# Loading the decay rates as one packet and spreading their logarithm by a matmul with ones, with k first on SyncE's queue

## The chip, the cores and the metric

The kernel runs on one core of a Trainium2 chip. The core has five engines that run side by side, each with its own instruction stream: TensorE (PE, matmul), VectorE (DVE), ScalarE (ACT), GpSimd (POOL) and SyncE (SP, which here only issues DMAs). They wait for each other through semaphores. The metric is the device time of one execution in microseconds (us), as the median of several runs. A profile is one further execution, recorded instruction by instruction.

## The reference

The program is a block-wise linear attention with a decay rate per head (`lam`, 8 numbers between 0.97 and 0.99), and behind it a two-layer network with the "snake" activation. Shapes: q, k and v are 4 x 8 x 768 x 64 (batch, head, position, dimension) in float32; the network takes 3072 tokens of 512 to 2048 and back to 512.

```python
Dmask = np.where(rel >= 0, lam[:, None, None] ** rel[None, :, :], 0.0)
for b in range(nb):                      # blocks of 64 positions
    intra = einsum('bhic,bhjc->bhij', qb, kb) * Dmask
    intra = einsum('bhij,bhjd->bhid', intra, vb)
    inter = einsum('bhid,bhde->bhie', qb * lam_pow, kv_state)
    out[:, :, sl] = intra + inter
    kv_state = lam_block * kv_state + einsum('bhsd,bhse->bhde', kb * rev_pow, vb)
h = x @ w_in                             # x: attention output, tokens x 512
s = np.sin(alpha * h)
g = h + s * s / (alpha + 1e-09)
return g @ w_out
```

## The kernel before

The kernel works on blocks of 128 positions (24 of them, six per batch) and on chunks of 512 tokens (six). Powers of lam are not put into a mask. They are multiplied into q and k: q of position p by lam^p, k by lam^-p, so that the mask that remains is 0 or 1. The factors are made once at the start. GpSimd writes the exponents (`E_i`, cast to `E_f`, lines 412 to 418), ScalarE takes `Ln` of lam (`lnlam`, line 438), VectorE multiplies the two (`lnL`, line 441), and ScalarE takes `Exp` into the tables `Lp`, `Lk` and `Lq` (lines 443 to 449). lam is loaded with a step of zero over 128 partitions (line 404), so every partition holds all 8 values. Three small activations load function tables: line 438 that of `Ln`, line 440 (`warm`) that of `Exp`, line 450 that of `Sin`, which the network needs.

The start, for the first four blocks, goes like this. SyncE's queue loads k and q (line 324, a helper that all loads share), then v, then the first quarter of `w_in` (`ws`). VectorE, and GpSimd for one of eight pieces, scale k (line 485) and q (line 468) into bf16. TensorE transposes them (lines 539 for q and 566 for k), ScalarE and VectorE copy the transposes out of PSUM (lines 544 and 577), TensorE makes the scores (line 618), VectorE masks them (`Sm`, line 629), and TensorE multiplies them with v (line 765) and adds the running state (`Zd`, lines 654, 672 and 785). The first matmuls of the network (line 862, then 828) come at about 19 us, and from there on attention blocks and network units are interleaved.

The order of the instructions on each engine is a fixed table of numbers (`_Plan.ORDER`): each number is an operation in the order in which the code makes them, and each engine works its row off from left to right, waiting on semaphores where an operation depends on another engine. In TensorE's row a pair such as `(64, 128)` is no operation of the kernel: it stands for 64 matmuls of 128 columns on a constant tile (`spin`, line 1140, whose operand is memset by VectorE on line 419 into a part of `Xs`). Their result is not used.

The lines on lam:

```python
load(lam_bc[:, :], bass.AP(lam.tensor, 0, [[0, 128], [1, H]]), "lam", 0.1, "lam", "SP", ...)
op("ACT", lambda e: e.activation(lnlam[:, :], lam_bc[:, :], ACTF.Ln), 0.25, ["lam"], ["lnlam"])
op("ACT", lambda e: e.activation(warm[:, :], lnlam[:, 0:1], ACTF.Exp, scale=0.0), 1.5, ["lnlam"], ["warm"])
op("DVE", lambda e: e.tensor_tensor(lnL[:, :, :], E_f[:, :, :], lnlam_b, ALU.mult), 0.46, ["E_f", "lnlam"], ["lnL"])
```

## Time and profile before

| what | value |
|---|---|
| time, median of 3 runs (lowest, highest) | 210.52 us (209.93, 210.64) |
| profiled execution: its time / its span from first to last instruction | 209.95 us / 208.2 us |
| busy share of TensorE, VectorE, ScalarE, GpSimd | 96%, 81%, 71%, 64% |
| granted TensorE clock, mean | 1.0 |
| moved by DMA | 34.40 MB in 83222 packets |

Times in the rows below are in us from the first instruction of the span, durations of one instruction in ns where a row says so. `PEld` is TensorE's loading of weights, `SPq` and `ACTq` are the issuing of DMAs by SyncE and ScalarE. In a row of the timeline the first number is the start and the second how long the group took from its first start to its last end; `x64` merges 64 instructions alike, and the bracket says how long the engine sat idle before it and what ended that.

### The profile page before, as it was taken

What the parts mean: (1) busy time and instruction counts of PE and PEld (TensorE: products, weight loads), DVE (VectorE), ACT (ScalarE), POOL (GpSimd) and SP (SyncE); (2) the same over time, 40 slices, a digit from 0 to 9 for tenths busy, and PEclk for the clock granted to TensorE, in tenths of its full rate; (3) what the DMA queues carried; (4) which work ended last, traced back from release to release, by engine and by line L of the source; (5) the groups of instructions that cost most, each with busy time, mean ns of one, the idle gap of its engine ahead of it and who ended that gap; (6) DMA issues with size and microseconds to landing.
All of it is one profiled execution on the core that took longest, in us unless ns stands there. A gap on an engine that the chain in (4) does not pass through costs nothing.

```text
span 208.2 us, 4897 instructions
## 1 busy us (share of the span) xinstructions
PE 200.0 (96%) x1972; PEld 136.8 (66%) x1972; DVE 168.5 (81%) x296; ACT 147.7 (71%) x270; POOL 132.4 (64%) x140
## 2 busy tenths in 40 slices
PE   6988999999997999998999999999999999999995
PEld 6756444557765877665657576665667666667994
DVE  2898567886989999987988979899798866767854
ACT  5658999448998999976979776898765579734300
POOL 6065689834968987954796850958851695585400
DMA  4999999999899999799997999380300004000324
GB/s 133 323 315 216 202 255 214 213 238 245 197 179 230 232 250 248 154 215 206 208 245 156 242 271 185 67 194 26 136 0 3 0 32 169 3 0 20 128 94 165
DMA packets 83222, 34.40 MB, mean 165 GB/s; under 512 B 59632, under 2 KB 80384, under 8 KB 83200
## 3 DMA queue, kind: packets, MB, share of 16 engines
q1 hardware_dynamic: 78544, 29.24, 62.5%
q0 software_dynamic: 3696, 3.67, 10.9%
q10 hardware_dynamic: 960, 1.19, 1.9%
q8 instruction: 15, 0.25, 0.5%
q14 instruction: 7, 0.06, 0.1%
HBM read 27.28 MB, written 6.29 MB: 161 GB/s over the span
## 4 chain that ended last, share of the span: by engine, by line
PE 79%; DVE 9%; ACT 4%; DMA 3%; SPq 2%; issue 1%; ACTq 1%; POOL 0%
PE bank L828 28%; PE bank L981 26%; PE bank L862 7%; PE bank L893 6%; PE bank L722 3%; PE bank L618 3%; DMA v<-in_v_dram 3%; SPq L324 2%; DVE gT L880 2%; DVE Sm L629 2%; DVE gT L845 2%; PE bank L700 1%; DVE w L936 1%; PE bank L654 1%; ACT Zd L672 1%; PE bank L662 1%
## 5 line engine op out<-in xcount | busy, mean ns | idle before, releaser
L828 PE MATMUL bank<-xT,w 128*128 128x512 bf16 x296 | 70.9, 380 | 1.0 <-ACT kept L1018 0.7
L845 DVE SCALAR_TENSOR_TENSOR gT<-u,rinv,bank 128x512 bf16<-128x512 bf16 x74 | 53.6, 744 | 18.2 <-ACT u L842 14.1
L838 ACT ACTIVATE t<-bank,alpha 128x512 bf16<-128x512 f32 x74 | 49.9, 683 | 19.9 <-PE bank L828 19.0
L828 PEld LDWEIGHTS bank<-xT,w 128*128 128x128 bf16 x296 | 27.8, 98 | 28.8 <-DVE gT L845 1.4
L959 POOL TENSOR_TENSOR gT<-gT 128x512 bf16<-128x512 bf16 x28 | 32.1, 1158 | 14.1 <-DVE Xs L959 8.9
L842 ACT ACTIVATE u<-t 128x512 bf16<-128x512 bf16 x57 | 35.2, 628 | 1.5
L843 POOL TENSOR_TENSOR u<-t 128x512 bf16<-128x512 bf16 x17 | 17.6, 1040 | 25.7 <-ACT t L838 25.7
L629 DVE TENSOR_TENSOR Sm<-bank,mask 128x1024 bf16<-128x1024 f32 x24 | 28.9, 1216 | 3.0 <-PE bank L618 1.1
L862 PE MATMUL bank<-xT,w 128*128 128x256 bf16 x176 | 21.6, 273 | 1.0 <-DVE gT L880 1.0
L880 DVE SCALAR_TENSOR_TENSOR gT<-u,rinv,bank 128x256 bf16<-128x256 bf16 x44 | 18.9, 474 | 4.2 <-ACT u L876 3.5
L959 POOL TENSOR_TENSOR Xs<-gT 128x512 bf16<-128x512 bf16 x19 | 21.8, 1162 | 0.3 <-DVE gT L845 0.3
L981 PE MATMUL bank<-w,gT 128*128 128x256 bf16 (+1 forms) x168 | 20.1, 268 | 0.0
L872 ACT ACTIVATE t<-bank,alpha 128x256 bf16<-128x256 f32 x44 | 18.5, 471 | 2.0 <-PE bank L862 1.7
L981 PE MATMUL bank<-ws,gT 128*128 128x256 bf16 x160 | 19.6, 273 | 0.0
L981 PE MATMUL bank<-w,Xs 128*128 128x256 bf16 (+1 forms) x168 | 19.5, 268 | 0.0
L478 POOL TENSOR_TENSOR qk<-q,Lq 128x512 bf16<-128x512 f32 x17 | 18.2, 1077 | 2.0 <-DMA q<-in_q_dram 2.0
L497 POOL TENSOR_TENSOR qk<-k,Lk 128x512 bf16<-128x512 f32 x16 | 17.4, 1090 | 3.3 <-DMA k<-in_k_dram 3.2
L862 PEld LDWEIGHTS bank<-xT,w 128*128 128x128 bf16 x176 | 16.3, 98 | 4.2 <-DVE gT L880 1.8
L981 PEld LDWEIGHTS bank<-w,gT 128*128 128x128 bf16 x168 | 15.9, 98 | 4.1 <-DVE gT L959 0.2
L981 PEld LDWEIGHTS bank<-w,Xs 128*128 128x128 bf16 x168 | 15.6, 98 | 3.3
L981 PEld LDWEIGHTS bank<-ws,gT 128*128 128x128 bf16 x160 | 15.3, 98 | 3.1 <-ACT xT L732 0.4
L893 PE MATMUL bank<-w,gT 128*128 128x512 bf16 x64 | 15.8, 380 | 0.0
(105 smaller groups left out, 266.0 us busy)
## 6 DMA issues: line engine op xcount, KB each, us to landing
k<-in_k_dram SPq DMA_DIRECT2D x24, 256.0 KB, 5.1
q<-in_q_dram SPq DMA_DIRECT2D x12, 512.0 KB, 6.2
v<-in_v_dram SPq DMA_DIRECT2D x24, 256.0 KB, 5.8
out_dram<-osb SPq DMA_DIRECT2D x18, 256.0 KB, 2.6
w<-in_moe_w_out_dram POOLq DMA_DIRECT2D x4, 512.0 KB, 7.8
w<-in_moe_w_in_dram POOLq DMA_DIRECT2D x3, 512.0 KB, 8.1
ws<-in_moe_w_in_dram SPq DMA_DIRECT2D x2, 512.0 KB, 7.5
out_dram<-osb ACTq DMA_DIRECT2D x8, 128.0 KB, 3.7
```

Of the source, the lines that this page charges most:

```text
L478: lambda e, a=a: e.tensor_tensor(qk2[:, j:j + 2, 4 * a:4 * a + 4, :], q32[:, jq, 4 * a:4 * a + 4, :, :].rearrange("p h t d -> p t h d"), b ...
L629: op("DVE", lambda e: e.tensor_tensor(Sm[js][:, :, :], banks[:, 512 * b0:512 * b0 + 1024].rearrange("p (c i) -> p c i", i=128), bass.AP(ma ...
L828: ins = e.matmul(ps[hb][:, c0:c1], w1[:, kc, 128 * m:128 * (m + 1)], xT[x][:, kc, c0:c1], start=(kc == 0 and c0 == lo), stop=(kc == NKC - ...
L838: op("ACT", lambda e: e.activation(t16[ju][:, w], ps[hb][:, w], ACTF.Sin, scale=alpha[:, m:m + 1]), 0.69 if hi - lo == TCH else 0.475, [ba ...
L842: lambda e: (e.activation(u16[ju][:, w], t16[ju][:, w], ACTF.Square) if e is nc.scalar else e.tensor_tensor(u16[ju][:, w], t16[ju][:, w], ...
L845: op("DVE", lambda e: e.scalar_tensor_tensor(out=gT[g][:, m, w], in0=u16[ju][:, w], scalar=rinv[:, m:m + 1], in1=ps[hb][:, w], op0=ALU.mul ...
L862: ins = e.matmul(ps[hb][:, 256 * i:256 * i + 256], w1[:, kc, 128 * (m + i):128 * (m + i + 1)], xT[x][:, kc, lo:lo + 256], start=(kc == 0 a ...
L872: op("ACT", lambda e, i=i: e.activation(t16[ju][:, 256 * i:256 * i + 256], ps[hb][:, 256 * i:256 * i + 256], ACTF.Sin, scale=alpha[:, m + ...
L880: op("DVE", lambda e, i=i: e.scalar_tensor_tensor(out=gT[g][:, m + i, lo:lo + 256], in0=u16[ju][:, 256 * i:256 * i + 256], scalar=rinv[:, ...
L893: ins = e.matmul(ps[ob][:, w], gT[g][:, m, 128 * s4:128 * (s4 + 1)], w2[:, m, w], start=(m == 0), stop=(m == NM - 1),)
L959: e.tensor_tensor(dst, in0, in1, alu), 0, rd, wr))
L981: ins = e.matmul(ps[ob][:, lo + d0:lo + d1], lhs, rhs[:, d0:d1], start=first and p == 0, stop=(p == NM // 2 - 1), skip_group_check=True)
```

## The change

lam is loaded into one partition (`lam_sb`, 1 x 8, one run of 32 bytes), and ScalarE issues that load as its first DMA, ahead of the load of alpha; SyncE's queue then begins with k. `Ln` works on one partition. A matmul of a row of 128 ones (new memset on VectorE) with the 8 logarithms writes them to all 128 partitions of PSUM bank 7, from where VectorE multiplies them with the exponents. Right behind the issue of alpha's load, ScalarE loads one table set that holds both `Ln` and `Exp`, so the `warm` activation for `Exp` goes; the one for `Sin` stays and now reads `lnL`. The fillers at TensorE's start are split into 14, the new matmul and 40. GpSimd casts `E_f` ahead of the mask work instead of behind some of it. A rule on what writes `ws` later in the kernel (line 935) is widened to both halves.

```diff
         "PE": (
-            (64, 128), 58, (5, 512), 60, 54, (11, 128), 38, 56, 52, 61, 66, 64, (1, 128), 68, 69, 74, 77,
+            (14, 128), 32, (40, 128), 59, (5, 512), 61, 55, (11, 128), 39, 57, 53, 62, 67, 65, (1, 128), 69, 70,
...
         "SP": (
-            0, 4, 3, 5, 2, 6, 7, 8, 9, 11, 10, 95, 96, 111, 108, 109, 110, 116, 112, 113, 121, 115, 114, 200,
+            4, 3, 5, 2, 6, 7, 8, 9, 11, 10, 96, 97, 112, 109, 110, 111, 117, 113, 114, 122, 116, 115, 201, 118,
...
-        lam_bc = sb("lam_bc", [128, H], F32)
-        lnlam = sb("lnlam", [128, H], F32)
+        lam_sb = sb("lam_sb", [1, H], F32)
+        lnlam = sb("lnlam", [1, H], F32)
+        ones = sb("ones", [1, 128], F32)
...
-            load(lam_bc[:, :], bass.AP(lam.tensor, 0, [[0, 128], [1, H]]), "lam", 0.1, "lam", "SP", lat=0.8, runs=1)
-            load(alphaT[:, :], bass.AP(moe_alpha.tensor, 0, [[128, NM], [1, 128]]), "alphaT", 0.1, "alphaT", "ACT", lat=2.0, runs=1)
+            load(lam_sb[:, :], bass.AP(lam.tensor, 0, [[H, 1], [1, H]]), "lam", 0.1, "lam", "ACT", lat=0.8, runs=1)
+
+            def load_alpha(e):
+                ins = e.dma_start(alphaT[:, :], bass.AP(moe_alpha.tensor, 0, [[128, NM], [1, 128]]))
+                e.preload_act_table_set("natural_log_exp_and_others")
+                return ins
+
+            op("ACT", load_alpha, 0.1, dma="alphaT", lat=2.0, issue=0.55, runs=1, writes=["alphaT"])
...
-            op("ACT", lambda e: e.activation(lnlam[:, :], lam_bc[:, :], ACTF.Ln), 0.25, ["lam"], ["lnlam"])
-            lnlam_b = bass.AP(lnlam, 0, [[H, 128], [0, 2 * NB + 4], [1, H]])
-            op("ACT", lambda e: e.activation(warm[:, :], lnlam[:, 0:1], ACTF.Exp, scale=0.0), 1.5, ["lnlam"], ["warm"])
+            op("DVE", lambda e: e.memset(ones[:, :], 1.0), 0.1, writes=["ones"])
+            op("ACT", lambda e: e.activation(lnlam[:, :], lam_sb[:, :], ACTF.Ln), 0.25, ["lam"], ["lnlam"])
+            op("PE", lambda e: e.matmul(ps[7][:, 0:H], ones[:, :], lnlam[:, :]), 0.3, ["ones", "lnlam"], [bank(7)])
+            lnlam_b = bass.AP(banks, 512 * 7, [[8 * 512, 128], [0, 2 * NB + 4], [1, H]])
             op("DVE", lambda e: e.tensor_tensor(lnL[:, :, :], E_f[:, :, :], lnlam_b, ALU.mult), 0.46,
-               ["E_f", "lnlam"], ["lnL"])
+               ["E_f", bank(7)], ["lnL"])
...
-            op("ACT", lambda e: e.activation(warm[:, :], lnlam[:, 0:1], ACTF.Sin, scale=0.0), 1.5,
-               ["lnlam", "Lk", "Lq", "Lq4", "Lp"], ["warm"])
+            op("ACT", lambda e: e.activation(warm[:, :], lnL[:, 0, 0:1], ACTF.Sin, scale=0.0), 1.5,
+               ["lnL", "Lk", "Lq", "Lq4", "Lp"], ["warm"])
...
-                        wr = [("T", i, x) for x in m] + ([("ws", 256 * (i // 3))] if i < 4 else [] if i == 4 else keys)
+                        wr = [("T", i, x) for x in m] + ([("ws", 0), ("ws", 256)] if i < 4 else [] if i == 4 else keys)
```

How the change moves instructions is best seen on three engines. On ScalarE, at the very start, before (the two loads of function tables and the `warm` between `Ln` and the first `Exp`):

```order
L324 DMA alphaT<-in_moe_alpha_dram 16x128
L438 ACT_TABLE_LOAD
L438 ACTIVATE lnlam<-lam_bc 128x8
L440 ACT_TABLE_LOAD
L440 ACTIVATE warm<-lnlam 128x1
L445 ACTIVATE Lp<-lnL 128x32
```

and ScalarE at the same place now:

```order
L325 DMA lam_sb<-in_lam_dram 1x8
L408 DMA alphaT<-in_moe_alpha_dram 16x128
L409 ACT_TABLE_LOAD
L446 ACTIVATE lnlam<-lam_sb 1x8 [waits dma_lam]
L453 ACTIVATE Lp<-lnL 128x32 [waits done_DVE]
```

One table load and one activation are gone between `lnlam` and `Lp`, and one DMA issue has come in ahead of the table load that remains. On TensorE, at its start, before (`Xs` is the constant tile of the fillers, `ident,qk` the transposes of q and k):

```order
L1140 MATMUL bank<-Xs 128x128 x64
L539 MATMUL bank<-ident,qk 128x128 x4
L1140 MATMUL bank<-Xs 128x512 x5
L566 MATMUL bank<-ident,qk 128x128 x4
L539 MATMUL bank<-ident,qk 128x128 x4
L1140 MATMUL bank<-Xs 128x128 x11
L453 MATMUL bank<-identf,alphaT 128x16
L539 MATMUL bank<-ident,qk 128x128 x8
```

and TensorE at the same place now, with its waits:

```order
L1148 MATMUL bank<-Xs 128x128 x13
L447 MATMUL bank<-lnlam,ones 128x8 [waits done_ACT]
L1148 MATMUL bank<-Xs 128x128 x40
L547 MATMUL bank<-ident,qk 128x128 [waits done_DVE]
L547 MATMUL bank<-ident,qk 128x128 x3
L1148 MATMUL bank<-Xs 128x512 x5
```

A row with one filler matmul of the same kind stands ahead of the first of these, so it is 14, the matmul that waits for ScalarE, and 40: 54 fillers in place of 64. On SyncE's queue, at its start, before (lam, then the first loads of k and q):

```order
L324 DMA lam_bc<-in_lam_dram 128x8
L324 DMA k<-in_k_dram 128x4x128
L324 DMA q<-in_q_dram 128x4x256
L324 DMA k<-in_k_dram 128x4x128
L324 DMA q<-in_q_dram 128x4x256
```

and SyncE's queue now:

```order
L325 DMA k<-in_k_dram 128x4x128
L325 DMA q<-in_q_dram 128x4x256
L325 DMA k<-in_k_dram 128x4x128
L325 DMA q<-in_q_dram 128x4x256
L325 DMA k<-in_k_dram 128x4x128 x2
```

Every load behind lam's stands one place further ahead; nothing else on this queue has moved.

## The prediction

> **What bounds the kernel now.** I read the page first, for where the time lies at all:

> ```profile
> span 208.2 us, 4897 instructions
> PE 200.0 (96%) x1972; PEld 136.8 (66%) x1972; DVE 168.5 (81%) x296; ACT 147.7 (71%) x270; POOL 132.4 (64%) x140
> PE 79%; DVE 9%; ACT 4%; DMA 3%; SPq 2%; issue 1%; ACTq 1%; POOL 0%
> ```

> TensorE is busy 96% of the span and carries 79% of the chain that ended last. The change touches only the first 8 us, so the question is by how much the first matmul of the network (19 us) moves; behind it TensorE runs nearly without a gap in a fixed order, and a shift there should reach the end.

> Next, the chain of waits within the first 30 us, in order of time (start, length, what):

> ```profile
> 0.81 0.40 SPq L324
> 1.25 0.42 SPq L324
> ...
> 6.35 6.02 DMA v<-in_v_dram
> 12.42 0.62 POOL v L491
> 13.09 0.62 PE bank L654 x8
> ...
> 16.93 1.05 ACT w L393
> 18.81 0.40 PE bank L785 x4
> 19.21 1.75 PE bank L862 x16
> ```

> The head begins with SyncE's issues, one behind the other, the first of them lam's, and then waits for the landing of v's second load. That is a chain of transfers. The second chain that I have to know runs over k, q and the scores; the timeline of the first 16 us shows it:

> ```profile
> 0.80 0.42 ACTq L324 DMA_DIRECT2D alphaT<-in_moe_alpha_dram  x1
> 0.90 0.17 DVE L426 MEMSET mask<- 128x128 bf16 x1 [0.90 <-PEq L1240]
> 1.25 1.28 ACT L438 ACT_TABLE_LOAD   x1 [1.25 <-PEq L1240]
> 1.66 5.60 PE L1140 MATMUL bank<-Xs 128*128 128x128 bf16 x64 [1.66 <-DVE Xs L419]
> 1.72 0.50 SPq L324 DMA_DIRECT2D q<-in_q_dram  x1
> 3.86 0.21 ACT L438 ACTIVATE lnlam<-lam_bc 128x8 f32<-128x8 f32 x1 [1.33 <-DMA lam_bc<-in_lam_dram]
> 4.09 1.28 ACT L440 ACT_TABLE_LOAD   x1
> 4.11 0.29 DVE L441 TENSOR_TENSOR lnL<-E_f,lnlam 128x128 f32<-128x128 f32 x1 [2.36 <-ACT lnlam L438]
> 5.68 0.23 ACT L445 ACTIVATE Lp<-lnL 128x32 f32<-128x32 f32 x1
> 5.95 0.69 DVE L485 TENSOR_TENSOR qk<-k,Lp 128x512 bf16<-128x512 f32 x1 [1.41 <-ACT Lp L445]
> 6.56 0.22 DVE L424 CAST ident<-identf 128x128 bf16<-128x128 f32 x1
> 6.69 1.29 DVE L468 TENSOR_TENSOR qk<-q,Lq 128x512 bf16<-128x512 f32 x2
> 7.43 0.40 PE L539 MATMUL bank<-ident,qk 128*128 128x128 bf16 x4 [0.17 <-DVE qk L468]
> 8.80 1.29 DVE L468 TENSOR_TENSOR qk<-q,Lq 128x512 bf16<-128x512 f32 x2 [0.21 <-DMA q<-in_q_dram]
> 9.90 0.23 PE L453 MATMUL bank<-identf,alphaT 16*128 16x16 f32 x1
> 10.07 0.73 PE L539 MATMUL bank<-ident,qk 128*128 128x128 bf16 x8
> 10.74 1.04 POOL L485 TENSOR_TENSOR qk<-k,Lp 128x512 bf16<-128x512 f32 x1 [5.46 <-DMA k<-in_k_dram]
> 11.72 0.64 PE L618 MATMUL bank<-qkT 64*64 64x128 bf16 x32 [0.70 <-ACT qkT L544]
> 12.18 4.62 DVE L629 TENSOR_TENSOR Sm<-bank,mask 128x1024 bf16<-128x1024 f32 x4 [0.37 <-PE bank L618]
> ```

> The scaling of k starts at 5.95, when `Lp` is there; that wait (1.41) is what lam's path costs. But at 8.80 VectorE waits again, for the second half of q, and at 10.74 GpSimd waits for k. From 8.80 on the transfers set the pace, and of lam's path only 0.21 us of idle time can be seen past that point. So two things count: when the stream of k, q and v starts, and whether TensorE's fillers, which stand in order ahead of the transposes, are through when the data are.

> **The change part by part.** The landing times, from the list of DMA issues (of the whole span, and of the moments at which k's and the two q's first loads are issued):

> ```profile
> lam_bc<-in_lam_dram SPq DMA_DIRECT2D x1, 4.0 KB, 3.0
> alphaT<-in_moe_alpha_dram ACTq DMA_DIRECT2D x1, 8.0 KB, 2.9
> out_dram<-osb SPq DMA_DIRECT2D x2, 64.0 KB, 1.7
> k<-in_k_dram SPq DMA_DIRECT2D x1, 256.0 KB, 3.6
> q<-in_q_dram SPq DMA_DIRECT2D x1, 512.0 KB, 4.7
> q<-in_q_dram SPq DMA_DIRECT2D x1, 512.0 KB, 6.0
> ```

> (1) *k first on SyncE's queue.* lam's issue stood from 0.81 to the start of k's at 1.25: every load behind it is issued 0.44 us earlier.

> (2) *128 packets become one.* DMA share from 1.6 to 2.4 us:

> ```profile
> q1 hardware_dynamic: 84, 0.01, 24.3%
> ```

> That is 84 packets in 0.243 x 16 x 0.8 = 3.1 us of engine time, 37 ns each, nearly all of them lam's of 32 bytes. All 128 are 4.7 us, or 0.30 us on each of 16 engines, ahead of k in the same queue. Removing them is worth between 0 (k's packets might not have been waiting) and 0.30 us. [...] The stream then moves by 0.44 to 0.74 us; I take 0.74.

> (3) *lam's path.* ScalarE's two issues of 0.42 run from 0.80 to about 1.68, the table load 1.28 to 2.98. lam lands between 0.80 + 1.7 = 2.5 (the small stores) and 0.80 + 3.0 = 3.8 (as before), so `Ln` ends at 3.2 to 4.05. The matmul has no row; the nearest is the float32 transpose at 9.90, 0.23 us. `lnL` adds 0.29 and `Lp` 0.23, with 0.03 at each hand-over: `Lp` is there at 4.05 to 4.9, against 5.91. The first k lands at 1.25 + 3.6 = 4.85, now 4.1 to 4.4. VectorE then scales k at 4.9 at the latest, to 5.6, casts `ident` (0.22) and has to wait for the first q: 1.72 + 4.7 = 6.42 less 0.74 is 5.7. So neither end of lam's landing matters on VectorE. The table load (1.28) and the activation (0.20) that go, 1.48 us on ScalarE's busiest early stretch, are covered by the transfer of q and count nothing of their own. [...]

> (4) *TensorE's fillers.* Their pace changes on the way (instructions seen in stretches of 0.2 us, one that straddles an edge counted on both sides):

> ```profile
> 4.80:5.00 0.20, 0.20 (x5) 0.20 (x3) 1.00 1.06 371
> 6.40:6.60 0.20, 0.20 (x8) 0.20 (x6) 1.00 1.11 371
> L1140 PE MATMUL bank<-Xs x83: 219/314/389, 1.7 to 14.3; 128*128 128x128 bf16 x76, 128*128 128x512 bf16 x7
> ```

> A record of 0.314 us is seen in a stretch for 0.2 + 0.314 us, so 5 of them are one every 0.10 us; later (0.2 + 0.22) / 8 is one every 0.053 us. The change of pace lies near 5.7 us, 4.0 us after the first filler: 38 at 0.105 and 26 at 0.055 make 5.4 and, with the last one's drain, the 5.60 of the row. The granted clock reads 1.00 throughout and does not show it. Now the memset of ones comes first (at most the 0.17 of a mask's), so 14 fillers run from 1.8 to 3.3; the matmul waits for `Ln` (3.2 to 4.05) and is through at 3.55 to 4.3; if the pace changes at 5.7 as before, 20 to 13 more fillers are slow and 20 to 27 fast, and the first transpose can start at 6.8 to 7.2. The scaled q is there at 5.7 + 0.69 = 6.4. So TensorE starts its transposes 0.2 to 0.6 us earlier than 7.43 and its fillers, not the data, are what it waits for. From 7.43 to the second group of transposes at 10.07 there are 2.64 us of work in order: that group now starts at 9.45 to 9.85, behind its q (landed at 2.81 + 6.0 = 8.81, now 8.07, scaled at 8.8). `S` (line 618) at 11.7 follows by 0.2 to 0.65, VectorE's side of it (two q, one k, three copies, 8.07 instead of 8.80) by 0.7. I take lam's early end, since a load of one packet is nearest to the small stores: 0.65.

> (5) *The rest.* `E_f` goes ahead on GpSimd, which sits idle for 5.46 us before 10.74: nothing. alpha is issued 0.44 later and lands near 4.2, used at 9.90: nothing. If those covers were gone they would cost 0.3 and 0.4. The widened rule on `ws` adds no wait on any engine. `Sin`'s table load moves ahead with `Exp`, and what ScalarE does behind it copies what TensorE has transposed.

> Sum: the v chain moves by 0.74 (GpSimd's cast at 12.42 waits for a landing), the score chain by 0.65. Both meet ahead of the network's first matmul, so the one that gains less counts. Against the profiled execution (208.2 of span and 1.75 around it, 209.95) that is 209.3; the median of the runs is 0.57 higher, 210.52, and less 0.65 it is 209.87, **209.9**.

> **The rivals.** *The pause resets the clock: slower.* TensorE now stands still between the 14th filler (3.3) and `Ln` if lam lands late. With lam at 3.8 the pause is 0.75 us. If TensorE then needs its 4.0 us of unbroken work again, all 40 fillers run at 0.105: 4.3 + 4.2 = 8.5 instead of 7.43, and everything behind it 1.1 later: 211.6. It decides from the point at which the first transpose comes later than 7.43. For it speaks that alpha's small load took 2.9; against it that work stood still for only a fifth of the time. [...]

> *The gain is hidden.* If packets of k, q and v are paced by something other than their start, or lam lands so late that only 0.2 comes through TensorE, the head moves by 0.2: 210.3. For it: the five 512-column fillers and the eleven after them stand in any case. Against it: two independent waits for transfers at 8.80 and 10.74.

> *The fillers cost more than in this profile.* The runs spread from 209.93 to 210.64 and the profiled one is at the low end. If in the slower ones the pace changes later, 64 fillers at 0.105 end at 8.4, and 54 end 10 x 0.105 = 1.05 earlier; with the matmul's 0.25 that leaves 0.8, and with the stream's gain, which is then freed too, up to 1.2: 209.3.

> **How the numbers follow.** This kernel's runs differ by 0.3% among themselves, 0.63 us, so faster means below 209.89 and slower above 211.15. The forecast (0.44 to 0.74 arrives, and the spread of the runs) has 0.66, with its own range from 209.5 to 210.2; its middle lies almost on the bound, so 0.36 of it counts as faster and 0.30 as no change. Fillers dearer: 0.14, faster. Hidden: 0.08, no change. The reset clock: 0.12, slower. Faster 0.50, same 0.38, slower 0.12. The range from 209.2 to 210.8 takes in the first three and leaves out most of the reset clock and the tails.

> **What would show it.** Right: k's first issue near 0.81; `Lp` before 5.0; the wait for q ahead of line 476 grown, as VectorE is now early; the first transposes near 6.8, line 626 near 11.0, the first network matmul near 18.4. Wrong: a gap in TensorE between the 14 fillers and line 447 with transposes after 7.43 (the clock), q's landing at 8.8 as before (the stream did not move), or the head earlier and the end not.

## The result, and the profile after

The changed kernel is slower: 213.0 us, median of six runs (212.56 to 213.58), against 210.33 us for the kernel before (six runs). The ratio is 1.0123, 95% interval [1.0092, 1.0153]. The profiled execution took 212.91 us, with a span of 210.9 against 208.2. Ratios leave out runs of more than 1.5% above a kernel's fastest and need not equal the quotient of two medians; some kernels below are held up only in part of their executions, and since this cuts off a part of the effect there, the mean granted clock of the runs is told as well. Of the six runs of the changed kernel four have a clock of 0.992 and two 1.00.

The page of the changed kernel, to be read against the first rows of the prediction:

```profile
span 210.9 us, 4879 instructions
PE 201.7 (96%) x1964; PEld 137.3 (65%) x1964; DVE 168.7 (80%) x297; ACT 146.5 (69%) x268; POOL 132.4 (63%) x140
PEclk9998899999999999999999999999999999999999
PE 82%; DVE 6%; DMA 4%; ACT 3%; issue 1%; ACTq 1%; POOL 0%
```

Two digits of 8 stand in the row of the granted clock, in the fourth and fifth slice of 5.3 us (16 to 26 us). The timeline of the changed kernel shows first what the change was made for, and then what happened at 16 us:

```profile
3.07 0.21 ACT L446 ACTIVATE lnlam<-lam_sb 1x8 f32<-1x8 f32 x1
3.40 0.59 PE L447 MATMUL bank<-lnlam,ones 1*128 1x8 f32 x2
4.35 0.23 ACT L453 ACTIVATE Lp<-lnL 128x32 f32<-128x32 f32 x1 [1.07 <-DVE lnL L449]
4.61 0.75 DVE L493 TENSOR_TENSOR qk<-k,Lp 128x512 bf16<-128x512 f32 x1 [0.16 <-ACT Lp L453]
7.19 0.39 PE L547 MATMUL bank<-ident,qk 128*128 128x128 bf16 x4
8.24 1.29 DVE L476 TENSOR_TENSOR qk<-q,Lq 128x512 bf16<-128x512 f32 x2 [0.80 <-DMA q<-in_q_dram]
9.81 0.73 PE L547 MATMUL bank<-ident,qk 128*128 128x128 bf16 x8
10.19 1.04 POOL L493 TENSOR_TENSOR qk<-k,Lp 128x512 bf16<-128x512 f32 x1 [4.66 <-ACT alpha L463]
11.46 0.64 PE L626 MATMUL bank<-qkT 64*64 64x128 bf16 x32 [0.70 <-ACT qkT L552]
15.83 0.23 PE L793 MATMUL bank<-qkT,Zd 128*128 128x128 bf16 x1
17.86 0.33 PE L793 MATMUL bank<-qkT,Zd 128*128 128x128 bf16 x3 [1.79 <-issue]
19.86 3.53 PE L870 MATMUL bank<-xT,w 128*128 128x256 bf16 x16
23.23 1.03 PE L836 MATMUL bank<-xT,w 128*128 128x512 bf16 x4
```

The kernel before, from 15 us on (line numbers are lower by 8):

```profile
16.09 0.40 PE L785 MATMUL bank<-qkT,Zd 128*128 128x128 bf16 x4
16.95 0.62 PE L654 MATMUL bank<-v,qk 64*128 64x128 bf16 x8 [0.47 <-ACT Zd L672]
18.81 0.40 PE L785 MATMUL bank<-qkT,Zd 128*128 128x128 bf16 x4 [0.34 <-ACT Zd L672]
19.04 1.91 PE L862 MATMUL bank<-xT,w 128*128 128x256 bf16 x16
20.79 1.03 PE L828 MATMUL bank<-xT,w 128*128 128x512 bf16 x4
```

The head did move: `Lp` from 5.68 to 4.35, the scaling of the second q from 8.80 to 8.24, the first score matmuls from 11.72 to 11.46. At 15.83 TensorE is 0.26 us ahead. Then it stops in the middle of four matmuls of one line, for 1.79 us, with no engine or transfer that it waits for ("issue"). Before, it waited 0.47 and 0.34 for ScalarE in this stretch; those waits are gone, so the pause costs 1.79 - 0.81 = 0.98. And the first 16 matmuls of the network take 3.53 instead of 1.91. The windows of the changed kernel say why (after the colon: length, then the busy time of PE, PEld, DVE, ACT and POOL with their instructions, the granted clock, the DMA share and GB/s):

```profile
16.00:18.00 2.00, 0.21 (x4) 0.14 (x2) 0.54 (x1) 1.66 (x3) 0.00 (x0) 1.00 1.25 211
18.00:20.00 2.00, 2.00 (x52) 1.58 (x51) 1.66 (x3) 0.73 (x2) 1.04 (x1) 0.94 1.25 207
20.00:22.00 2.00, 2.00 (x12) 1.33 (x11) 1.04 (x4) 1.54 (x3) 0.00 (x0) 0.50 1.25 211
22.00:24.00 2.00, 2.00 (x11) 1.18 (x9) 0.00 (x0) 1.22 (x4) 0.00 (x0) 0.71 1.18 193
```

After the stretch in which TensorE hardly worked, the granted clock goes to 0.50 and is back by 24. The account of the two profiled executions:

| place | after minus before, us |
|---|---|
| last matmul ahead of the pause (15.83 for 16.09) | -0.26 |
| pause of 1.79, less the waits of 0.81 that it replaces | +0.98 |
| the rest up to the network (a remainder) | +0.10 |
| first network matmul (19.86 for 19.04) | +0.82 |
| those 16 matmuls at half clock (3.53 for 1.91) | +1.62 |
| line 836 (23.23 for 20.79) | +2.44 |
| end of the span (210.9 for 208.2) | +2.7 |

The last 0.26 arise later and were not followed. The account is that of one execution: the two runs whose clock was 1.00 took 212.74 and 213.51, as long as the others, and what they lost in place of the halved clock stands in no trace.

What TensorE may have waited for shows in the list of DMA queues (packets, MB, share of 16 engines). Queue q8 is named "instruction"; on the page of the changed kernel it has

```profile
q8 instruction: 15, 0.25, 0.5%
```

over the whole span, 0.02 MB a packet. The first of them in the kernel before lies in the window from 11 to 12 us:

```profile
q8 instruction: 1, 0.02, 7.2%
```

and in the changed kernel in that from 15 to 16 us, with none earlier:

```profile
q8 instruction: 1, 0.02, 7.0%
```

Taken in narrower windows the packets start at 11.36 and 15.48. I take this queue for TensorE's: from the fourth packet to the fifteenth (53.48 to 198.21 in the changed kernel, 51.07 to 195.84 in the one before) both traces have 1366 matmuls, 1366 weight loads and 26 waits of TensorE, 251 instructions for each of the eleven packets, while VectorE has 297 and ScalarE 268 in the whole span of the changed kernel. Some records can be missing, so 251 is an estimate. In the kernel before there is no pause of TensorE near its first packet, in this one there is.

**Theory A**: each packet brings TensorE a block of instructions; taking ten fillers out of its stream moves the borders of these blocks to other places of the program, the next block comes late there, TensorE pauses, and the clock falls behind the pause. **Rival B**: lam's new path (issue on ScalarE, matmul, one table set) or the transfers that now start earlier cause the delay in some way; the fillers don't matter but for their time.

### The profile page after: what moved, and what is told of

It is laid out like the page before. It is cut to its first block, busy times and chain, and to the rows that moved or that the text cites. A ratio compares the mean times of both kernels' runs of the same rounds, so it can differ in the third digit from the quotient of the medians.

```text
span 210.9 us, 4879 instructions
## 1 busy us (share of the span) xinstructions
PE 201.7 (96%) x1964; PEld 137.3 (65%) x1964; DVE 168.7 (80%) x297; ACT 146.5 (69%) x268; POOL 132.4 (63%) x140
## 4 chain that ended last, share of the span: by engine, by line
PE 82%; DVE 6%; DMA 4%; ACT 3%; issue 1%; ACTq 1%; POOL 0%
PE bank L836 27%; PE bank L989 26%; PE bank L870 8%; DMA w<-in_moe_w_out_dram 4%; PE bank L1148 4%; PE bank L901 3%; PE bank L626 3%; PE bank L730 3%; DVE gT L888 2%; PE bank L708 1%; DVE gT L853 1%; DVE Sm L637 1%; ACT t L846 1%; PE bank L662 1%; DVE w L944 1%
## 5 line engine op out<-in xcount | busy, mean ns | idle before, releaser
L836 PEld LDWEIGHTS bank<-xT,w 128*128 128x128 bf16 x296 | 27.8, 98 | 29.4 <-ACT kept L1026 1.8
L870 PE MATMUL bank<-xT,w 128*128 128x256 bf16 x176 | 23.2, 286 | 0.1
L870 PEld LDWEIGHTS bank<-xT,w 128*128 128x128 bf16 x176 | 17.1, 102 | 4.2 <-DVE gT L888 0.9
L989 PEld LDWEIGHTS bank<-w,Xs 128*128 128x128 bf16 x168 | 15.6, 98 | 3.3
L901 PE MATMUL bank<-w,gT 128*128 128x512 bf16 x64 | 15.8, 380 | 0.2 <-DMA w<-in_moe_w_out_dram 0.2
## 6 DMA issues: line engine op xcount, KB each, us to landing
k<-in_k_dram SPq DMA_DIRECT2D x24, 256.0 KB, 5.5
q<-in_q_dram SPq DMA_DIRECT2D x12, 512.0 KB, 5.9
v<-in_v_dram SPq DMA_DIRECT2D x24, 256.0 KB, 5.2
out_dram<-osb SPq DMA_DIRECT2D x18, 256.0 KB, 2.6
w<-in_moe_w_out_dram POOLq DMA_DIRECT2D x4, 512.0 KB, 8.2
w<-in_moe_w_in_dram POOLq DMA_DIRECT2D x3, 512.0 KB, 9.0
ws<-in_moe_w_in_dram SPq DMA_DIRECT2D x2, 512.0 KB, 6.4
```

The source lines that it names most:

```text
L836: ins = e.matmul(ps[hb][:, c0:c1], w1[:, kc, 128 * m:128 * (m + 1)], xT[x][:, kc, c0:c1], start=(kc == 0 and c0 == lo), stop=(kc == NKC - ...
L870: ins = e.matmul(ps[hb][:, 256 * i:256 * i + 256], w1[:, kc, 128 * (m + i):128 * (m + i + 1)], xT[x][:, kc, lo:lo + 256], start=(kc == 0 a ...
L901: ins = e.matmul(ps[ob][:, w], gT[g][:, m, 128 * s4:128 * (s4 + 1)], w2[:, m, w], start=(m == 0), stop=(m == NM - 1),)
L989: ins = e.matmul(ps[ob][:, lo + d0:lo + d1], lhs, rhs[:, d0:d1], start=first and p == 0, stop=(p == NM // 2 - 1), skip_group_check=True)
```

## Experiments: ten fillers, or lam's path

*The change with 64 fillers instead of 54.*

```diff
-            (14, 128), 32, (40, 128), 59, (5, 512), ...
+            (24, 128), 32, (40, 128), 59, (5, 512), ...
```

> The changed kernel with ten fillers put back ahead of the new matmul (24 and 40 in place of 14 and 40), nothing else. Theory A: the pause of 1.8 us on TensorE at 16 us, which ends with nothing that the profile names, is a wait for the next 16 KB of TensorE's own instructions; ten fillers fewer (twenty instructions) put the request for that block behind more of the transfers of the network's weights. Then putting them back brings the block early again: its packet near 11 us in place of 15.4, no pause at 16 us, granted clock 1.00 from 18 to 24 us, and the time about that of the kernel before or up to 0.4 us below it (209.9 to 210.5), the shorter head now counting. Theory B: the pause belongs to lam's new path (the matmul into bank 7, the split fillers and the clock they leave behind); then it stays, and the time stays near 213.0.

Measured 211.15 us against 210.46, ratio 1.0005 [0.9976, 1.0035]. Everything else of the change is in, and the slowdown is gone. No pause, first q8 packet at 11.30, clock 1.00 in all ten runs.

*The kernel before with 54 fillers instead of 64.*

```diff
-            (64, 128), 58, (5, 512), ...
+            (54, 128), 58, (5, 512), ...
```

> The kernel before with 54 fillers in place of 64 and nothing of the change. Theory A (instruction block requested later): the packet of the first instruction block comes late, at 14 to 16 us in place of 11.3, TensorE pauses for 1 to 2 us near 16 us, the granted clock falls near 20 us, and the time is 212 to 213.5. Theory B (lam's new path): no pause, time 209.9 to 210.6.

Measured 212.3, ratio 1.0085 [1.0046, 1.0124]; 4 of the 9 runs have a clock of 0.992 or less. Nothing of lam's path is in it, and the pause is there in its profile (of the slowest of the nine runs). TensorE's waits in its first 30 us:

```profile
PE bank L785 <- issue: 1.8, 1, 1.8
```

Its q8 packet starts at 16.05, and the windows show a clock of 0.85, 0.50 and 0.79 from 18 to 24 us. So the ten fillers are enough by themselves, and B falls.

*The change with the 50 fillers behind the matmul (64 in all, otherwise placed).*

```diff
-            (14, 128), 32, (40, 128), 59, (5, 512), ...
+            (14, 128), 32, (50, 128), 59, (5, 512), ...
```

> The changed kernel with 14 and 50 fillers (64 in all, the ten put behind the new matmul instead of ahead of it). Theory A: as with 24 and 40, packet near 11.3, no pause, time as before within 0.5 us (209.9 to 210.9), since ten more fillers hold the transposes back by 0.5 to 1 us. Theory B (the early matmul and what it leaves of the clock): pause and 213.

Measured 211.83, ratio 1.0056 [1.003, 1.0082]; no pause, packet at 12.30, clock 1.00 in all ten runs. It lies above the kernel with 24 and 40, and its profile starts the first transposes late (8.50); on that below.

*lam's load, still one packet, first on SyncE's queue.*

```diff
         "ACT": (
-            0, 1, ...
+            1, ...
         "SP": (
-            4, 3, ...
+            0, 4, 3, ...
```

> The changed kernel with lam's load of one packet put back as the first of SyncE's queue, so that k, q, v and the weights are issued about 0.4 us later again; the table set, the matmul and the fillers as changed. Theory A, in which the place of the request among the transfers decides: the weights' loads are again issued as in the kernel before while the request is about 0.3 us later than there, so the block may come early (no pause, near 210.3) or late (pause, near 213); the packet's time and the pause go together either way. Theory B (lam's new path alone): pause and 213.0 as in the changed kernel.

Measured 213.04, ratio 1.0086 [1.0045, 1.0127], with the pause (1.86 at line 793) and the packet at 15.86: the place of lam's issue does not matter for it.

*The kernel before, with lam's 128 packets issued by ScalarE and k first on SyncE's queue.*

```diff
         "ACT": (
-            1, ...
+            0, 1, ...
         "SP": (
-            0, 4, 3, ...
+            4, 3, ...
```

> The kernel before with one part of the change: lam's load, still 128 packets, is issued by ScalarE, so that k is first on SyncE's queue; 64 fillers, two table loads, no matmul. Prediction's step 1 alone: transfers 0.44 us earlier, time 0.2 to 0.5 us below before (210.0) if nothing else moves. Theory A allows that the weights' loads, now 0.4 us earlier against an unchanged TensorE, get ahead of the request for instructions: then the packet comes at 14 to 16 us, with a pause near 16 us and 212 to 213.5. Theory B: no pause, near 210.0.

Measured 211.15, ratio 1.0017 [0.9987, 1.0047]: no gain. There lam lands later (`Ln` starts at 4.52 instead of 3.86), `Lp` starts at 6.34, the first transposes wait for q until 8.09 and the scores start at 12.37. k first on its queue, with the rest as it was, moves the delay to lam.

## Experiments: the place of the block's border

In each trace with such a pause, counting TensorE's matmuls from the start (line 447 as two) gives 221 ahead of it. This fits a border that lies at a fixed number of instructions. Going back by one block (matmuls, their weight loads, separate waits) I get to about the 97th matmul with the 251 instructions estimated above, and to about the 95th with the 256 that the expectations take. In the changed kernel that is among the four transposes of k right ahead of the first score matmuls, which wait for ScalarE, and in the kernel before with 54 fillers at the end of them; with 64 it is within, or one ahead of, the eight transposes of q before them. If only the number counts, ten fillers anywhere ahead of that wait must cure it, and ten right behind it must not.

*Ten fillers ahead of the first score matmuls, in TensorE's idle 0.70 us, and, as a control, ten right behind them.*

```diff
-            ... 39, 57, 53, 62, 67, 65, ...
+            ... 39, 57, 53, 62, (10, 128), 67, 65, ...
```

```diff
-            ... 39, 57, 53, 62, 67, 65, ...
+            ... 39, 57, 53, 62, 67, (10, 128), 65, ...
```

> The changed kernel with its 54 fillers at the start as they are, and ten more put right ahead of the first score matmuls (line 626), where TensorE stood idle for 0.7 us for ScalarE's copies. By counting back 256 instructions from the place of the pause, the block's border lies in the last transposes ahead of those matmuls in all kernels with 54 fillers, and 2 to 11 matmuls earlier with 64. Theory A2 (the request goes out a few instructions behind the border; with 54 fillers the wait of the score matmuls, until 11.4 us, comes in between): now ten fillers follow the border without a wait, so the packet comes near 11 to 12 us, no pause at 16 us, clock 1.00 from 18 to 24 us, and with the head 0.3 us or more ahead of the kernel before the time is 209.6 to 210.4. Theory A1 (the border itself asks, and the packet then queues behind transfers): border and transfers are as in the changed kernel, so the packet stays at 15 to 16 us, and the pause grows, since the ten fillers are in the block: 213 to 214.

> The control: the same ten fillers, put behind the first group of score matmuls instead of ahead of it, so that the total is 64 too. Theory A2: the wait of the score matmuls still lies between the border and the request; packet at 15 to 16 us, pause near 16 us of 1.8 us or more, 212.5 to 214. A theory in which the count of fillers or the work that they give TensorE matters, and not their place: no pause, as with 64 at the start, 209.9 to 211.

Ahead: 210.58, ratio 1.0001 [0.9973, 1.0029], packet at 12.81, no pause, and the network's first matmuls at full clock:

```profile
18.99 1.91 PE L870 MATMUL bank<-xT,w 128*128 128x256 bf16 x16
```

Behind: 212.46, ratio 1.0099 [1.0063, 1.0134], packet at 16.34, and the pause has come ten matmuls earlier in the program:

```profile
17.01 0.53 PE L773 MATMUL bank<-Sm,v 64*64 64x128 bf16 x23
18.95 0.33 PE L773 MATMUL bank<-Sm,v 64*64 64x128 bf16 x9 [1.41 <-issue]
```

After the change 32 of line 773 and one of 793 stood ahead of the pause, here 23: again 221. The two kernels have the same instructions and differ in the place of ten. This shows A: the place in the stream decides, not the work that the ten do. In the control's profile, and in 5 of its 6 runs, the clock stayed at 1.00, and it is slow all the same. (That profile also came late to its first transposes, at 8.15 for 7.40 with the ten ahead, so the comparison of times rests on the medians and not on the two profiles.)

*Four fillers ahead of them.*

```diff
-            ... 39, 57, 53, 62, 67, 65, ...
+            ... 39, 57, 53, 62, (4, 128), 67, 65, ...
```

> The changed kernel with four more fillers ahead of the first score matmuls in place of ten. With none there the packet of the next instruction block came at 15.42 and TensorE paused for 1.8, with ten it came at 12.73 and TensorE did not pause. If the request for the block goes out at most eight instructions behind the border (which four matmuls with their weight loads now put ahead of the wait): packet near 12.7, no pause, 210.6. If it goes out further behind it: packet near 15.4 to 15.8, a pause of 1.5 to 1.8, and 212 to 213. If the ten fillers of the other run helped by keeping TensorE busy and not by their number: the pause and the clock drop remain, 212 or more, with the packet early all the same.

Measured 211.08 against 210.91, ratio 1.0036 [1.0003, 1.0069]; in the profile the packet starts at 12.70 and there is no pause, but 3 of the 10 runs have a clock of 0.992. So four do most of what ten do, not in every execution.

## Experiments: why the block is late

*The loads of `ws` one place later in SyncE's order (in the changed kernel), and one place earlier (in the kernel before).*

```diff
-            ... 9, 11, 10, 96, 97, 112, 109, ...
+            ... 9, 11, 10, 112, 96, 97, 109, ...
```

```diff
-            ... 9, 11, 10, 95, 96, 111, 108, ...
+            ... 9, 11, 95, 96, 10, 111, 108, ...
```

> The changed kernel with the two loads of the first network weights (512 KB each) issued one place later on SyncE's queue, behind a load of k of 256 KB; TensorE's stream untouched, 54 fillers. In all five profiles so far the block's packet came at 11.3 to 11.6 us where VectorE had scaled the second half of q, for which TensorE waits ahead of that place, 0.2 us before the weights' first load was issued, and at 15.4 to 16.0 where it was 0.3 to 0.4 us after. Theory A1 (the block queues behind the weights' loads): the packet comes near 11.5, no pause, and the time is 1 to 2.5 us below the changed kernel's 213.0, less up to 0.8 for the later weights, so 210.5 to 212. Theory A2 (only the place in TensorE's stream decides, whatever is issued): packet at 15 to 16, pause, 213 to 214.

> The kernel before, with 64 fillers, and the two weights' loads issued one place earlier on SyncE's queue, ahead of the last load of v. Theory A1 (the block queues behind the weights' loads): they are issued near 8.8 us, before TensorE gets to the place at 9.5, so the packet comes late, at 14.5 to 16 us, with a pause near 16 us and a fall of the clock: 212 to 214. Theory A2 (only the place in the stream): packet near 11.3, no pause; the last piece of v lands 1 to 2 us later and costs at most that: 210.5 to 212.

Later: the packet comes at 13.39 and the pause shrinks to 0.42, but then TensorE waits 1.11 for ScalarE, which waits for the `ws` that is now late, and the clock still falls (to 0.50 in the profile; 3 of the 10 runs have 0.992); 211.34, ratio 1.0041 [1.0014, 1.0067]. Earlier: the packet comes at 11.25, as in the kernel before, and there is no such pause; the time of 214.26, ratio 1.019 [1.0123, 1.0257], has another cause, v's last load, which now lands late (ScalarE waits for it until 18.16, and TensorE for ScalarE's `Zd`; all 4 runs have a clock of 0.992 or less):

```profile
PE bank L654 <- ACT Zd L672: 2.5, 1, 2.5
```

So the block does not simply queue behind `ws`. My second thought was that the request goes out some instructions behind the border and is held by the wait of the score matmuls: where the pause was 1.4 or more, the packet started 3.9 to 4.1 us after these (15.48 for 11.46; 16.05 for 11.99; 16.34 for about 12.4). Four fillers in between were indeed enough in the profile. But a kernel of the next section has ten or twelve matmuls between border and wait, and its packet comes at 15.11, 4.1 after the scores too. That thought falls or is not all of it; what delays the packet stays open.

## Experiments: where the gain of the head went

Even without the pause the changed kernel equals the one before (1.0001, 1.0005), where I had expected 0.65 us less. Either TensorE's fillers hold the gain, or the data.

Three kernels meant for this had an edit that left one matmul in every group of fillers (it was to make some of them 32 x 32); their expectations speak of the edit as intended.

```diff
-                    ins = e.matmul(ps[0][:, 0:cols], idle[:, 0:128], idle[:, 0:cols])
+                    r = 32 if cols == 32 else 128
+                ins = e.matmul(ps[0][0:r, 0:cols], idle[:, 0:r], idle[:, 0:cols])
```

> The changed kernel with 54 very small fillers (32 columns on 32 columns of weights) in place of the 14 ahead of the new matmul; the 40 behind it stay. TensorE then has issued its 190th instruction near 6 us instead of 10 us, at about the same end of the fillers. Theory A (the block of instructions is requested when TensorE gets to a fixed place in its stream, and the block waits behind what has been issued by then): its packet comes before 11 us, no pause at 16 us, clock 1.00 from 18 to 24 us, the shorter head counts, time 209.6 to 210.4, at or below the kernel before. Theory B (the number of fillers matters through TensorE's clock, not through the place in the stream): the small fillers keep TensorE no busier than the 14 did, so pause and loss stay, 212 to 213.

> The changed kernel with 30 fillers behind the new matmul instead of 40, and 20 very small ones (32 columns on 32 columns of weights) ahead of the first score matmuls, so that the border of the instruction block is followed by 12 matmuls without a wait, as in the kernel before. Theory A2: no pause, packet at 11 to 13 us. In addition, theory F (TensorE's fillers, not the transfers, have held the head since q lands earlier): the first transposes start near 6.6 instead of 7.2 to 7.4, line 626 near 11.0 to 11.3, and the time is 0.3 to 0.6 us below the kernel before, 209.9 to 210.3 where before is 210.6. Theory G (fewer fillers leave TensorE at its slow pace for longer): transposes at twice the time, line 626 no earlier than 11.7, 210.6 to 212.5.

> The changed kernel with the early fillers kept (14 and 40) and those between the transposes cut (4 of 512 columns instead of 5, 3 of 128 instead of 11), and 20 very small ones ahead of the first score matmuls. Theory A2: no pause. Theory F: the second group of transposes starts 0.7 us earlier, 9.1 to 9.3, line 626 near 11.0, time 0.3 to 0.6 us below the kernel before (209.9 to 210.3 where before is 210.6). Theory G: the pace stays slow longer in some runs, and the time is 210.6 to 212.

As built they tell what the fillers are for. Medians 212.38, 212.46 and 212.83; ratios 1.0055 [1.0021, 1.0089], 0.9955 [0.991, 1.0001] (from 3 runs of 12) and 1.0133 [1.0097, 1.0168]. Those three runs of the second kernel, 208.24, 209.09 and 210.28, are far below its other nine (211.65 to 213.74), and none of them was profiled. In the first kernel the transposes start at 6.37, and yet the network starts 1.4 us later than before:

```profile
6.37 0.61 PE L547 MATMUL bank<-ident,qk 128*128 128x128 bf16 x4 [2.22 <-DVE qk L476]
12.15 1.07 PE L626 MATMUL bank<-qkT 64*64 64x128 bf16 x32 [0.52 <-DVE qkT L585]
20.46 1.80 PE L870 MATMUL bank<-xT,w 128*128 128x256 bf16 x15
```

The scores take 1.07 instead of 0.64, and TensorE keeps this slow pace until 16 us, in the profiles of the other two until after 22. With one filler in a group TensorE comes to its full pace no earlier than 15.6 us; with all of them it has it by 8.4 us in every profile.

*Ten fillers fewer ahead of the transposes* and *one of 512 and eight of 128 columns fewer between them*, each with twenty small ones ahead of the scores so that the count of instructions is that of the cure above:

```diff
-            (14, 128), 32, (40, 128), 59, ... 62, 67, 65, ...
+            (14, 128), 32, (30, 128), 59, ... 62, (20, 32), 67, 65, ...
```

```diff
-            ... 59, (5, 512), 61, 55, (11, 128), 39, 57, 53, 62, 67, 65, ...
+            ... 59, (4, 512), 61, 55, (3, 128), 39, 57, 53, 62, (20, 32), 67, 65, ...
```

> Thirty fillers of 128 columns in place of forty ahead of the first transposes, and twenty of 32 columns ahead of the first score matmuls, so that TensorE's instruction stream holds ten more matmuls ahead of them, as in the run with ten fillers there (210.58). If TensorE's fillers held the gain of the shorter head: the first transposes (line 547) near 6.6 instead of 7.4, the first score matmuls (626) near 11.2 instead of 11.67, and 210.1 or less. If something else holds it (the transfers of q and k, or a slow pace that lasts until TensorE has worked for a set time): 626 at 11.5 to 11.8 again and 210.4 to 210.8. If the stream's blocks are not what matters but the count of long fillers: a pause of 1.8 at line 793 or near it, and 212.5.

> The fillers ahead of the first transposes as in the changed kernel (14 and 40), but behind them one of 512 columns and eight of 128 fewer, and twenty of 32 columns ahead of the first score matmuls. If the fillers between the transposes held the gain: the first transposes at 7.2 to 7.4, the second group (547 x8) near 9.2, held by its q (9.0) from there on, line 626 near 11.0 and 209.9 to 210.2. If the data hold it: the second group at 9.7, 626 at 11.5 or later and 210.4 to 210.8. A pause at line 793 is expected by neither, since the stream holds eleven more matmuls ahead of the score matmuls.

Ratios 1.0003 [0.9969, 1.0037] and 0.999 [0.9952, 1.0029]; medians 211.18 and 212.06 against 210.91. In both profiles the scores are early, 11.02 and 11.01, so TensorE's fillers did hold the gain. The second one's profile carries it to the network, in spite of a short pause:

```profile
11.01 0.64 PE L626 MATMUL bank<-qkT 64*64 64x128 bf16 x32
15.84 0.35 PE L773 MATMUL bank<-Sm,v 64*64 64x128 bf16 x10 [0.51 <-issue]
18.33 1.91 PE L870 MATMUL bank<-xT,w 128*128 128x256 bf16 x16
```

This is 0.71 ahead of the kernel before at the first network matmul. The first one's profile loses it again:

```profile
14.96 0.53 PE L773 MATMUL bank<-Sm,v 64*64 64x128 bf16 x23
17.64 0.32 PE L773 MATMUL bank<-Sm,v 64*64 64x128 bf16 x9 [2.15 <-issue]
```

The late block comes and goes from one execution of the same kernel to the next: 4 of 12 runs of the one and 7 of 12 of the other have a clock of 0.992 or less (the second kernel's expectation of the last pair says 6), and they reach 214.57 and 214.75, while the best runs are 209.7 and 208.95. I had expected no pause in either.

*The same two, with 22 small fillers ahead of the eight transposes of q*, so that the border lies near these as in the kernel before (by the two counts above one to four matmuls ahead of the first of them):

```diff
-            (14, 128), 32, (40, 128), 59, (5, 512), 61, 55, (11, 128), ...
+            (14, 128), 32, (30, 128), 59, (5, 512), 61, 55, (22, 32), (11, 128), ...
```

```diff
-            ... 59, (5, 512), 61, 55, (11, 128), ...
+            ... 59, (4, 512), 61, 55, (22, 32), (3, 128), ...
```

> The kernel with thirty fillers ahead of the first transposes again, but with its small fillers (22 of 32 columns) ahead of the second group of q's transposes (547 x8) and not behind it, so that the border of TensorE's first 256 instructions lies inside that group, as in the kernel before. If the place of the border decides whether the next block comes in time: no pause near line 773 or 793 and a granted clock of 1.00 in nearly all runs (with the small fillers behind the group, 4 of 12 had 0.992 or less), line 626 near 11.0 to 11.2, and a median near 209.9, the time that the six fastest runs had with them behind. If lateness goes with the earlier head itself (TensorE is earlier than the transfer of its code, wherever the border lies): pauses in about half of the runs again and 211.2 or more.

> The kernel with one filler of 512 columns and eight of 128 fewer between the transposes, with its small fillers (22 of 32 columns) ahead of the second group of q's transposes. If the place of the border decides: a granted clock of 1.00 in nearly all runs (behind the group, 6 of 12 had 0.992 or less), line 626 near 11.0 to 11.2, a median of 209.8 to 210.3. If lateness goes with the earlier head: pauses in about half of the runs and 211.5 or more.

The clock is 0.992 or less in 1 of 12 and 2 of 12 runs, against 4 and 7, and neither profile has a pause. Counted over the five experiments with the border at the transposes of q (without the one whose `ws` is early, which loses the clock behind another wait), 3 of 54 runs have the lower clock; with 54 fillers and nothing added, 16 of 25 (the changed kernel, the one before with 54, and the one with lam on SyncE). The lower clock only stands in for the pause here: the control had the pause without it. That the border's place alone made the difference in this last pair is not shown, because in both profiles the head is not early any more (line 626 at 12.76 and 12.54), so TensorE also had more time until it needed the block. The time of the head does not decide by itself, though: with nothing added ahead of the wait the pause is there with line 626 at 11.99 and 12.42 too, and with four or ten fillers there it is missing at 11.39 and 11.67.

The times are 211.34, ratio 1.0042 [1.0013, 1.0071], and 211.59, 1.0028 [0.9992, 1.0065]: the early head is lost in another way. The 22 small fillers now stand in TensorE's row ahead of q's transposes and no longer in its idle time: from the transposes of 4 to those of 8 it is 1.84 and 1.40, against 1.09 and 0.64 with the small fillers behind, about 0.75 more in both. And in the first one's profile TensorE still ran at its slow pace at 7.09 (four transposes in 0.63 instead of 0.39):

```profile
7.09 0.63 PE L547 MATMUL bank<-ident,qk 128*128 128x128 bf16 x4
9.26 0.39 PE L547 MATMUL bank<-ident,qk 128*128 128x128 bf16 x4
9.57 1.44 PE L1149 MATMUL bank<-Xs 128*32 128x32 bf16 x33
12.76 0.64 PE L626 MATMUL bank<-qkT 64*64 64x128 bf16 x32 [0.70 <-ACT qkT L552]
```

What delays the packet is open, but how late is too late can be read from all traces but the three with one filler in a group. In the seven with a pause TensorE comes to the place behind matmul 221 between 0.1 and 2.2 us after the packet's start and goes on 2.4 to 2.9 us after it (17.86 for 15.48 in the changed kernel, 18.95 for 16.34 in the control, 15.84 for 13.12 where the pause was 0.51). In the nine without one it comes there 2.5 us or more after the packet's start: 2.5 and 2.7 in the last pair, 2.9 with the four and the ten, 4.5 or more with 64 fillers. So the packet and the pause belong together in every one of them.

No version tried beats the kernel before by more than can be measured.

## Why the prediction was wrong

- **The step that failed is (4), the fillers**, with the sentence ahead of it that behind the head TensorE runs nearly without a gap and a shift reaches the end. I took ten fillers fewer as time alone. They are also 20 instructions with their weight loads, and the sum had no term for what moves when 20 instructions leave TensorE's stream: the next block of it came at 15.48 instead of 11.36, and that cost 0.98 of pause and 1.62 of halved clock in the profile. That the fillers' number and place do this is shown by the pair of ten fillers ahead of and behind the wait, and by both kernels with the other number of fillers; why the block comes late there stays open.
- **Terms (1) and (2), the stream**: bounds 0.44 to 0.74, taken 0.74, measured 0.56 (second q) and 0.55 (k on GpSimd, whose wait the changed kernel's profile puts down to ScalarE). k's issue gave its 0.44; for the second q this leaves about 0.1 to the 128 packets, not 0.30. No run shows that lam's packets go ahead of k's as a whole, which the 0.30 takes for granted: in the kernel before k's packets start at 2.3, and between 3.2 and 3.4 us 22 of the 110 packets are still under 512 bytes. The first k and the first q, which the sum did not rest on, gained more than the bounds: issue and time to landing give 0.81 + 3.0 = 3.8 for 4.85 and 1.32 + 4.0 = 5.3 for 6.4.
- **Term (3), lam's path**, was right: `Lp` at 4.35, inside 4.05 to 4.9, and not on the path; `Ln` found lam there at 3.07. The matmul, priced at 0.23 from a float32 transpose, took 0.59 with two records, and it stands in TensorE's row ahead of the 40 fillers. The 0.21 us of idle time at 8.80 that the prediction gave to lam's path is a wait for q.
- **The rest of (4)**: first transposes forecast for 6.8 to 7.2, measured 7.19 (6.93 to 7.50 in the changed kernel's other versions with 14 and 40 that were quick to change pace); second group 9.45 to 9.85, measured 9.81. Both came at the late end, since the pace changed at 6.1 and not at 5.7, and the scores gained 0.26, not 0.65. This term was too large even without the pause: with the ten fillers ahead of the wait the ratio is 1.0001. Line 626 at 11.0 took nine or ten fillers less.
- **Term (5)**: in the rows above `E_f`, alpha, the rule on `ws` and `Sin`'s table load delay nothing; they were not tried one by one.
- **The rival of the reset clock** named the clock, but at the wrong place: `Ln` ended at 3.28, the 14 fillers were just through, and line 447 started at 3.40 without a gap. The clock fell at 19.8.
- **The rival of the dearer fillers** exists in single executions: where the pace changes late, the first transposes come at 8.42 to 8.50 with 64 fillers (8.4 was worked out) and at 8.15 and 8.16 with 54. It did not decide.

## What to carry to other kernels

Ten fillers taken out moved all later instructions of TensorE against the packets of the instruction queue, one of which came at 15.48 instead of 11.36, and the kernel was slower by a ratio of 1.0123. When a harmless edit costs more than its own time, look for a gap that ends with "issue" in the middle of a run of like instructions (1.79 us here), and for the times of the instruction queue's packets; here ten dummy matmuls ahead of a wait cured it (ratio 1.0001) and four mostly did (1.0036). And read the granted clock behind a gap on TensorE: here the slow stretch after it cost 1.62 us and the gap 0.98.

## What the runs showed of the hardware

```profile
16.34:19.76 3.42, 1.90 (x50) 1.48 (x50) 1.63 (x4) 2.08 (x4) 1.04 (x1) 1.00 1.25 207
14.95:18.36 3.41, 2.37 (x67) 1.47 (x66) 2.65 (x3) 2.57 (x7) 1.54 (x3) 1.00 1.24 248
```

- The pace at the start changes (in the changed kernel from a filler every 0.107 us to one every 0.056, at 6.1) at the first entry of the same list: at 4.6 to 6.7 us in ten traces, at 7.5 to 8.4 in five, and at 15.6, 22.5 and 23.3 with one filler in a group. Kernels with the same instructions up to there differ in it (5.78 and 8.39; 6.55 and 8.18), so the instructions alone do not set it. The views show 1.00 ahead of the first entry, so their 1.00 at the start says nothing of the clock.
- The float32 matmul of one row of 128 ones by 8 columns has two records and took 0.59 us at the slow pace. The load of 32 bytes in one packet, issued at 0.81, was there when `Ln` started at 3.07.
